# Attention plus MLP on one core: the softmax's running maximum over the first 512 keys, with a check and a second program behind it

## The chip, the core and the metric

The kernel runs on one core of a Trainium2 chip. The metric is device time in microseconds. The core's engines run their own instruction streams and meet through semaphores: TensorE (PE, with its weight loads as PEld), VectorE (DVE), ScalarE (ACT), GpSimd (POOL), and SyncE (SP), whose queue issues all the transfers here.

## The reference

One input `x` of 2048 rows of 448 is normalized row by row, and the normalized rows go through an attention with 16 query heads and a single key and value head of 28 columns, and through an MLP. The output is the sum of `x` and both:

```
xn = layernorm(x)
q = (xn @ wq), 16 heads of 28;  k = xn @ wk;  v = xn @ wv
p = softmax(q k^T * 28**-0.5)            # over 2048 keys
a = (p v, heads joined) @ wo
m = relu(xn @ w1) @ w2                   # 448 -> 1792 -> 448
out = x + a + m
```

The inputs are normal numbers of spread 0.05. A softmax does not change when any one number is taken off a row's scores, as long as the exponentials stay in range. The row's maximum is the usual choice of that number.

## The kernel before, in words

Everything stays in one program without loops at run time. Three stages follow each other.

*Projections.* `x` is normalized and transposed, and q, k and v are computed for four blocks of 512 rows. Each float32 operand is split into a high and a low part, and several matmuls make up for the precision. q, k and v are written to a scratch tensor in DRAM (`qscr`).

*MLP.* The hidden 1792 columns are cut into 7 parts of 256, each over 4 row blocks: 28 tasks (`mlp_up`, `mlp_down`). Max tiles of the attention are mixed into the later tasks, one at each of 12 places of a task (`between`, `one_max`). `LEAD` says how many go here.

*Attention.* The work is cut into 16 units (`NU`): a block of 512 queries by a group of 4 heads. For a unit, a stack `qst` [128, 4, 512] is loaded from `qscr` (`load_stack`: one transfer of zeros and four of q). Its first 112 partitions hold q as high and low parts against the same parts of k in `kst`. Two more partitions hold the negated row maxima as high and low parts against ones in `kst`, so the score matmul itself subtracts the maximum. There are five stack buffers, and unit u + 4 is loaded at the start of unit u, into the buffer that unit u - 1 has given up.

Three kinds of matmul fill TensorE there:

- A **max tile** (`max_tile`, L353): 128 queries by 512 keys of one head into a PSUM bank of the ring `psM` (tile `m`, 4 banks), which VectorE reduces to a row's maximum (L357). Four key blocks, four query blocks and four heads make 64 tiles a unit, 1024 in all. When a unit has all of them, `max_all` and `max_rows` negate, split, transpose and write them into the unit's stack.
- A **score** (`score`, L593): 128 keys by 512 queries of one head into a bank of the ring `psA` (tile `a`, 3 banks), of which ScalarE takes the exponential into a tile `p` (L595). 64 a unit, 1024 in all.
- The products **with v** (`pv`, L477): the four heads of a key block side by side in the array's columns, accumulated over a unit's 16 key blocks in one bank (`psO`). A ones column in `vtile` gives the denominator as row 28 of each head. The trace has two records for each of these 1024 matmuls.

The denominators go by transfer into a tile `d`, are inverted (`recips`), spread and multiplied in (`normalized`), and after each four units the output projection runs (`o_proj`, L530), the last block's in pieces (`o_proj_part`, L546; `finish`).

The order in attention is written by a planner at build time (the loop at the end). It keeps a modelled clock for TensorE (`t`), ScalarE (`act`) and VectorE (`dve`) and the time at which each bank comes free, and it picks next a score, a max tile, a group of v products or an output projection. It paces the max tiles over the scores (`due`, `SLACK`), asks only whether a stack's load has been ordered (`mx_todo[0][0] in qst`), and has no time for transfers. A score takes a bank of `psA`, and one of `psM` only when no max tile is left.

Of the kernel before, what the change touches and what calls it, by code (L numbers as in the profile page):

```python
# [7 lines left out]

F32 = mybir.dt.float32
F32R = mybir.dt.float32r  # L10
AF = mybir.ActivationFunctionType
ALU = mybir.AluOpType
AX = mybir.AxisListType
# [4 lines left out]

@with_exitstack
def attention_plus_mlp(ctx: ExitStack, tc: tile.TileContext, x, wq, wk, wv, wo, w1, w2, out):
    nc = tc.nc
    P = 128
    S, D = x.shape
    DH = wk.shape[1]
# [3 lines left out]
    QB = 512  # L30
    NQB = S // QB
    TPB = QB // P
    HG = 4
# [13 lines left out]
    NU = NQB * NHG  # L47
    NA, NM = 3, 4
    assert DR == 64 and KQ + 2 <= P and HG * 32 == P and NPART * FP == DFF

    ctx.enter_context(tc.manual_schedule())
    cst = ctx.enter_context(tc.tile_pool(name="cst", bufs=1))
    small = ctx.enter_context(tc.tile_pool(name="small", bufs=2))
    dram = ctx.enter_context(tc.tile_pool(name="dram", bufs=1, space=DRAM))
# [12 lines left out]
    vtile = cst.tile([P, NKB, 32], F32, name="vtile")  # L67
# [5 lines left out]
    eps_t = cst.tile([P, 1], F32, name="eps_t")  # L73
    nc.vector.memset(eps_t, EPS)
    warm = cst.tile([P, 1], F32, name="warm")

    pw = psM.tile([P, QB], F32, name="m")
    for _ in range(WARM):
# [243 lines left out]
    def v_rows():  # L322

        pv = psM.tile([P, QB], F32, name="m")
        for kb in range(NKB):
            nc.tensor.transpose(pv[:, kb * 32 : kb * 32 + DH], vT[0][:, kb * P : (kb + 1) * P], ident[0:DH, 0:DH])
        nc.vector.tensor_copy(vtile[:, :, 0:DH], pv.rearrange("p (i d) -> p i d", d=32)[:, :, 0:DH])


    qst, nmx, mx_todo = {}, {}, []  # L330
# [10 lines left out]
            src = qscr[g, r % 2, 0:MQ, b * QB : (b + 1) * QB].rearrange("(j d) q -> d j q", d=DH)  # L341
            nc.sync.dma_start(st.bitcast(F32)[r * DH : (r + 1) * DH], src)

    mx_todo = [(u, j, s, h) for u in range(NU) for j in range(HG) for s in range(TPB) for h in range(4)]

    def max_tile():

        u, j, s, h = mx_todo.pop(0)
        if u not in nmx:
            nmx[u] = small.tile([P, HG * TPB, 4], F32, name="nmx")  # L350
        pm = psM.tile([P, QB], F32, name="m")
        k0 = h * QB
        nc.tensor.matmul(  # L353
            pm, qst[u][0:KQ, j, s * P : (s + 1) * P], kst[0:KQ, k0 : k0 + QB], start=True, stop=True
        )
        n = j * TPB + s
        nc.vector.tensor_reduce(nmx[u][:, n, h : h + 1], pm, axis=AX.X, op=ALU.max)  # L357
        return u if n == HG * TPB - 1 and h == 3 else None

    def max_all(u):  # L360

# [53 lines left out]

    LEAD, PER = 192, 12
    tasks = [(p, b) for p in range(NPART) for b in range(NQB)]
    FIRST = len(tasks) - LEAD // PER  # L420
    pending = []

    def one_max():
        done = max_tile()
        if done is not None:
            pending.append((n + 1, done, max_all(done)))

# [18 lines left out]
        mlp_down(*tasks[-1], i)  # L446
    while pending:
        max_rows(*pending.pop(0)[1:])
    assert len(mx_todo) == NU * HG * TPB * 4 - LEAD
    mlp.close()  # L450


# [51 lines left out]
    def recips(u):  # L504

        r = opool.tile([P, EQ], F32, name="r")
        nc.vector.reciprocal(r, o_r[u])
        nc.sync.dma_start(rscr[u].rearrange("j (g e) -> (j g) e", e=EQ), r)
        rb = opool.tile([P, QB], F32, name="rb")
        for j in range(HG):  # L510
            nc.sync.dma_start(rb[32 * j : 32 * j + 32], rscr[u, j : j + 1].to_broadcast([32, QB]))
        o_r[u] = rb
# [37 lines left out]
    def finish(u):  # L550

        b, g = units[u]
        o = o_acc.pop(u)
        cols = [slice(i * P, (i + 1) * P) for i in range(TPB)]
        oS = opool.tile([P, QB], F32, name="oS")
        on = opool.tile([P, QB], F32, name="on")
        r = opool.tile([P, TPB, HG, 1], F32, name="r")
        rb = opool.tile([P, TPB, HG, 32], F32, name="rb")
        pt = [psA.tile([P, QB], F32, name="a") for _ in cols]
        for i, c in enumerate(cols):  # L560
            nc.scalar.activation(oS[:, c], o[:, c], AF.Copy)
        for i, c in enumerate(cols):
            nc.tensor.transpose(pt[i][:, 0:P], oS[:, c], ident)
            dens = pt[i][:, 0:P].rearrange("p (j c) -> p j c", j=HG)[:, :, DH : DH + 1]
            nc.vector.reciprocal(r[:, i], dens)
            nc.gpsimd.tensor_scalar(rb[:, i], r[:, i].to_broadcast([P, HG, 32]), 1.0, 0.0, op0=ALU.mult, op1=ALU.add)
        for i, c in enumerate(cols):
            pb = psM.tile([P, QB], F32, name="m")
            nc.tensor.transpose(pb[:, 0:P], rb[:, i].rearrange("p j c -> p (j c)"), ident)
            nc.vector.tensor_tensor(on[:, c], pb[:, 0:P], oS[:, c], op=ALU.mult)  # L570
        for i, c in enumerate(cols):
            t = b * TPB + i
            py = psA.tile([P, QB], F32, name="a")
            nc.tensor.matmul(py[:, 0:D], on[:, c], g3[:, g, :], start=True, stop=True)
            nc.vector.tensor_tensor(acc[:, t, :], py[:, 0:D], acc[:, t, :], op=ALU.add)
            nc.sync.dma_start(out[t * P : (t + 1) * P, :], acc[:, t, :])

# [25 lines left out]
    while n_s < n_all or blocks:  # L605
        step = n_s // HG
        room = n_s < n_all and n_open < P_BUFS
        n_max = left - len(mx_todo)
        due = min(left, n_s * left // spread_over)
        wants = mx_todo and n_max < due + SLACK and mx_todo[0][0] in qst  # L610
        rest = rings["M"][0] - t
        pool = "M" if not mx_todo and not fill and rings["M"][0] < rings["A"][0] else "A"
        wait_s = max(0, rings[pool][0] - t) if room and (n_max + SLACK >= due or not wants) else None
        wait_m = max(0, rest) if wants else None
        n_v = ready()
        tail = NKB - blocks[0][1] if blocks else 0
        if n_v < tail <= MIN_V + 1 and room:
            n_v = 0
        least = min((w for w in (wait_s, wait_m) if w is not None), default=None)
        if least == 0:  # L620
            if wait_s == 0 and wait_m == 0:
                what = "S" if act <= dve else "M"
            else:
                what = "S" if wait_s == 0 else "M"
        elif fill and rest <= WAIT and (not mx_todo or what != "F"):
            what = "F"
        elif n_v >= MIN_V or n_v >= 2 and (least is None or least > WAIT) or n_v and (n_s == n_all or not room):
            what = "V"
        elif wait_s is None and wait_m is None:
            if not n_v:  # L630
                t = max(blocks[0][3], t if blocks[0][1] else acc_free)
            what = "V"
            n_v = max(1, ready())
        else:
            what = "S" if wait_m is None or wait_s is not None and wait_s <= wait_m else "M"
        if what == "V" and fill and (len(fill) > 4 * TPB or n_s == n_all and n_v == len(blocks)):
            what = "F"
        if what == "S":
            t = max(t, rings[pool][0])
            assert n_s // (HG * NKB) not in nmx  # L640
            u, kb, p = score(pool)
            n_s += 1
            n_open += 1
            act = max(act + T_EXP, t + TO_ACT)
            rings[pool] = rings[pool][1:] + [act + ACT_OUT]
            t += T_MM
            ps.append(p)
            if len(ps) == HG:
                blocks.append((u, kb, ps, act + ACT_OUT))
                ps = []  # L650
                if kb == 0 and u:
                    load_stack(u + 4)
                for f, a in side.pop(step, ()):
                    f(*a)
        elif what == "M":
            t = max(t, rings["M"][0])
            done = max_tile()
            dve = max(dve + T_MAX, t + TO_DVE)
            rings["M"] = rings["M"][1:] + [dve + DVE_OUT]
            t += T_MM  # L660
            if done is not None:
                dve += T_MAX
                at(step + 1, max_rows, done, max_all(done))
        elif what == "V":
            for u, kb, pp, _ in blocks[:n_v]:
                pv(step, u, kb, pp)
                t += T_PV
                n_open -= HG
                if kb == NKB - 1:
                    act = max(act, t) + T_EXP  # L670
                    acc_free = act + ACT_OUT
            t += T_MODE
            blocks = blocks[n_v:]
        else:
            f, a = fill.pop(0)
            f(*a)
            t = max(t, rings["M"][0]) + 3 * NHG * T_PROJ
            dve = max(dve, t) + T_MAX
            rings["M"] = rings["M"][1:] + [dve + DVE_OUT]
# [26 lines left out]
```

## Time and profile before

| | |
|---|---|
| median of three runs | 1136.87 us (1136.49 to 1138.59) |
| span of the profiled execution, first to last instruction | 1136.1 us |
| first score to last product with v | 389.9 to 1125.5 us |
| TensorE, VectorE, ScalarE busy | 1122.3, 792.7, 589.7 us |
| max tiles on TensorE, reductions on VectorE | 1024, 1024 |
| mean granted clock of TensorE | 0.999 |

The profiled execution is known by its span, 0.8 us under the median; device time is that of the whole execution. Times in the profile count from the span's start. A group's mean is the length of one instruction from its start to its modelled end, and matmuls overlap in the array, so the price of a matmul is read from the distance of the starts.

### The profile page before, as it was taken

To read this page: it belongs to the slowest core of one execution; us is meant where nothing else is said; L and a number is where in the kernel's file an instruction comes from. 1 tells how busy PE (TensorE), PEld (TensorE's weight loads), DVE (VectorE), ACT (ScalarE), POOL (GpSimd) and SP (SyncE) were. 2 spreads that over 40 slices of the span, in tenths; PEclk is the share of its full clock that TensorE was granted. 3 is DMA by queue.
4 is the path that set the end of the run, shared out by engine and by line. 5 is a ranking of instruction groups with operands and counts; after the bars stand their busy time and mean duration, and the time that the engine had idled before them with its cause. 6 is when DMAs were issued, how large, how long until landed. Compare 5 with 4: busy or idle time off the path is not lost.

```text
span 1136.1 us, 15337 instructions
## 1 busy us (share of the span) xinstructions
PE 1122.3 (99%) x5908; PEld 754.4 (66%) x5908; DVE 792.7 (70%) x1385; ACT 589.7 (52%) x1175; POOL 112.7 (10%) x97
## 2 busy tenths in 40 slices
PE   8899999999999999999999999999999999999998
PEld 7688888888888855555556565555665555665553
DVE  6633346888888887788777787777777778767401
ACT  5421111000110277777776676676667767756893
POOL 2204022020200020010110101101010110101110
PEclk9999999999999999999999999999999999999999
DMA  6673810001000102022022110202202020000000
GB/s 217 223 186 68 167 47 1 1 1 36 1 1 1 30 1 48 1 47 39 11 47 49 24 38 18 47 7 50 55 10 52 5 47 9 11 28 9 11 10 33
DMA packets 38478, 47.90 MB, mean 42 GB/s; under 512 B 10294, under 2 KB 25046, under 8 KB 38238
## 3 DMA queue, kind: packets, MB, share of 16 engines
q1 hardware_dynamic: 38406, 46.93, 16.9%
q8 instruction: 46, 0.75, 0.3%
q14 instruction: 26, 0.21, 0.1%
HBM read 32.37 MB, written 12.18 MB: 39 GB/s over the span
## 4 chain that ended last, share of the span: by engine, by line
PE 93%; ACT 3%; DVE 2%; DMA 1%; issue 1%; SPq 0%; DVEq 0%; ACTq 0%
PE m L353 21%; PE a L593 21%; PE o L477 20%; PE a L169 11%; PE a L407 9%; PE o L407 3%; PE m L530 3%; PE a L174 2%; ACT p L595 2%; PE m L593 1%; DMA qscr<-qs 1%; DVE st L182 1%; DMA stg<-in_A_wq 1%; PE m L546 0%; DVE qs L237 0%
## 5 line engine op out<-in xcount | busy, mean ns | idle before, releaser
L357 DVE TENSOR_REDUCE nmx<-m 128x1 f32<-128x512 f32 x1024 | 633.3, 682 | 148.9 <-PE m L353 148.0
L595 ACT ACTIVATE p<-a 128x512 f32<-128x512 f32 x969 | 495.5, 644 | 174.2 <-PE a L593 174.0
L353 PE MATMUL m<-kst,qst 112*128 112x512 f32 x1024 | 407.1, 401 | 0.0
L593 PE MATMUL a<-qst,kst 128*128 128x512 f32 x969 | 388.7, 408 | 0.8 <-ACT p L595 0.5
L593 PEld LDWEIGHTS a<-qst,kst 128*128 128x128 f32 x969 | 183.1, 189 | 117.9 <-issue 55.3
L477 PE MATMUL o<-p,vtile 128*32 128x512 f32 x2048 | 238.6, 596 | 0.0
L353 PEld LDWEIGHTS m<-kst,qst 112*128 112x128 f32 x1024 | 193.8, 189 | 52.2 <-DVE nmx L357 11.4
L394 ACT ACTIVATE hH<-a 128x512 fp32r<-128x512 f32 x56 | 33.5, 598 | 267.4 <-PE a L174 143.0
L477 PEld LDWEIGHTS o<-p,vtile 128*32 128x32 f32 x2048 | 57.6, 109 | 130.6 <-issue 125.1
L169 PE MATMUL a<-xH,w 128*128 128x512 f32 x414 | 112.0, 393 | 3.1 <-ACT xH L225 2.3
L407 PE MATMUL a<-w,hH 128*128 128x448 f32 x336 | 96.0, 367 | 0.0
L169 PEld LDWEIGHTS a<-xH,w 128*128 128x128 f32 x414 | 77.4, 188 | 20.0 <-ACT xH L225 3.1
L395 DVE SCALAR_TENSOR_TENSOR hL<-a,hH 128x512 fp32r<-128x512 f32 x56 | 38.7, 692 | 69.6 <-ACT hH L394 69.6
L516 POOL TENSOR_TENSOR on<-rb,oS 128x512 f32<-128x512 f32 x15 | 19.4, 1292 | 645.7 <-ACT p L595 353.5
L407 PEld LDWEIGHTS a<-w,hH 128*128 128x128 f32 x336 | 63.6, 189 | 8.6
L169 PE MATMUL a<-xL,w 128*128 128x512 f32 x207 | 63.9, 392 | 0.0
L414 DVE TENSOR_TENSOR acc<-a,acc 128x448 f32<-128x448 f32 x84 | 51.8, 618 | 14.8 <-PE a L407 14.8
L407 PE MATMUL a<-w,hL 128*128 128x448 f32 x168 | 61.4, 365 | 0.0
L169 PEld LDWEIGHTS a<-xL,w 128*128 128x128 f32 x207 | 38.9, 188 | 8.8 <-DVE xL L226 0.3
L174 PE MATMUL a<-xR,w 128*128 128x512 f32 x138 | 42.6, 390 | 0.2 <-DVE xR L231 0.2
L595 ACT ACTIVATE p<-m 128x512 f32<-128x512 f32 x55 | 36.2, 741 | 7.0 <-PE m L593 7.0
L407 PEld LDWEIGHTS a<-w,hL 128*128 128x128 f32 x168 | 31.6, 188 | 2.5
(104 smaller groups left out, 539.4 us busy)
## 6 DMA issues: line engine op xcount, KB each, us to landing
qst<-qscr SPq DMA_DIRECT2D x64, 224.0 KB
qscr<-qs SPq DMA_DIRECT2D x16, 512.0 KB
rb<-rscr SPq DMA_DIRECT2D x60, 64.0 KB
acc<-in_A_x SPq DMA_DIRECT2D x16, 224.0 KB
out<-acc SPq DMA_DIRECT2D x16, 224.0 KB
stg<-in_B_w SPq DMA_DIRECT2D x7, 448.0 KB
stg<-in_B_w SPq DMA_DIRECT2D x7, 384.0 KB
qst<-zeros SPq DMA_DIRECT2D x16, 112.0 KB
```

The costliest lines, as they stand in the source:

```text
L169: nc.tensor.matmul(ps, lhs[:, wi, c, cols], xm[:, c, xs], start=n == 0, stop=False)
L174: nc.tensor.matmul(ps, lhs[:, wi, DC, cols], xR[:, xs], start=False, stop=wi == 1)
L353: nc.tensor.matmul(pm, qst[u][0:KQ, j, s * P : (s + 1) * P], kst[0:KQ, k0 : k0 + QB], start=True, stop=True)
L357: nc.vector.tensor_reduce(nmx[u][:, n, h : h + 1], pm, axis=AX.X, op=ALU.max)
L394: nc.scalar.activation(hH[:, f], ph, AF.Relu)
L395: nc.vector.scalar_tensor_tensor(hL[:, f], ph, 0.0, hH[:, f].bitcast(F32), op0=ALU.max, op1=ALU.subtract)
L407: nc.tensor.matmul(py[:, 0:D], hm[:, f, i * P : (i + 1) * P], wd[:, wi, f, :], start=n == 0, stop=n == 3 * FC - 1)
L414: nc.vector.tensor_tensor(acc[:, t, :], py[:, 0:D], acc[:, t, :], op=ALU.add)
L477: nc.tensor.matmul(o_acc[u][32 * j : 32 * j + 32], vtile[:, kb, :], p, start=kb == 0, stop=kb == NKB - 1)
L530: nc.tensor.matmul(py[:, 0:D], om[:, i * P : (i + 1) * P], wm[:, g, :], start=n == 0, stop=n == 3 * NHG - 1)
L593: nc.tensor.matmul(pt, kst[:, kb * P : (kb + 1) * P], qst[u][:, j, :], start=True, stop=True)
L595: nc.scalar.activation(p, pt, AF.Exp, scale=SCALE)
```

## The change

The maximum is taken over the first 512 keys only: `HM` = 1 key block instead of 4, so 16 max tiles a unit and 256 in all. What is subtracted then may be smaller than a row's true maximum. The program sums up what could have gone out of range: all denominators (`dsum`, and `gone` in `finish`), and 1e5 times the largest absolute v. One matmul with a column of ones adds that over the partitions, and a comparison with 1e20 gives an integer `fine`. Every engine reads `fine` into a register. If it is zero, the whole program runs again from the inputs with `HM` = 4, that is, as before. The second program stands behind the first in the code. If `fine` is not zero, every engine branches past it.

Three more things follow from `HM`. `LEAD` falls from 192 to 80 max tiles ahead of attention, which are now five units' tiles instead of three, put into tasks 21 to 27 instead of 12 to 27. A score may take a bank of `psM` at any time (`spare`). And the planner paces 176 max tiles over the scores where it paced 832.

```diff
+def attention_plus_mlp(ctx: ExitStack, tc: tile.TileContext, *io):
...
+    program(tc, 1, fine, *io)
+    flag = nc.values_load(fine, skip_runtime_bounds_check_because="it is only compared with zero")
+    with tc.If(flag == 0):
+        program(tc, 4, None, *io)
...
+            nc.vector.tensor_reduce(
+                gone[:, TPB : TPB + 1], vtile[:, :, 0:DH], axis=AX.XY, op=ALU.max, apply_absolute_value=True
+            )
...
-    mx_todo = [(u, j, s, h) for u in range(NU) for j in range(HG) for s in range(TPB) for h in range(4)]
+    mx_todo = [(u, j, s, h) for u in range(NU) for j in range(HG) for s in range(TPB) for h in range(HM)]
...
-    LEAD, PER = 192, 12
+    LEAD, PER = min(192, 5 * HG * TPB * HM), 12
...
+            nc.vector.tensor_tensor(dsum, dsum, o_r[u], op=ALU.add)
...
+                nc.vector.tensor_reduce(gone[:, i : i + 1], dens, axis=AX.XY, op=ALU.add)
...
+            nc.vector.tensor_reduce(gone[:, TPB + 1 : TPB + 2], dsum, axis=AX.X, op=ALU.add)
+            nc.vector.scalar_tensor_tensor(
+                gone[:, TPB + 1 : TPB + 2], gone[:, TPB : TPB + 1], 1e5, gone[:, TPB + 1 : TPB + 2],
+                op0=ALU.mult, op1=ALU.add,
+            )
+            nc.vector.tensor_reduce(gone[:, TPB : TPB + 1], gone[:, 0:TPB], axis=AX.X, op=ALU.add)
...
+            nc.tensor.matmul(pg[0:1, 0:1], gone[:, TPB : TPB + 1], gone[:, TPB + 2 : TPB + 3], start=True, stop=True)
+            nc.vector.tensor_scalar(fine, pg[0:1, 0:1], 1e20, None, op0=ALU.is_le)
...
-        pool = "M" if not mx_todo and not fill and rings["M"][0] < rings["A"][0] else "A"
+        spare = HM == 1 or not mx_todo and not fill
+        pool = "M" if spare and rings["M"][0] < rings["A"][0] else "A"
```

The change moves instructions. In the order of TensorE after the change (the lines there are 377 for a max tile, 635 for a score, 501 for v, 572 for the last output projection), the place where unit 1 begins: `qst_1279`, `qst_1285` and `qst_3224` are the stacks of units 0, 1 and 5.

```order
L635 MATMUL a_3204<-qst_1279,kst_130 128x512
L635 MATMUL a_3208<-qst_1285,kst_130 128x512
L635 MATMUL a_3212<-qst_1285,kst_130 128x512
L635 MATMUL m_3216<-qst_1285,kst_130 128x512
L635 MATMUL m_3220<-qst_1285,kst_130 128x512
L377 MATMUL m_3231<-kst_130,qst_3224 128x512
L377 MATMUL m_3234<-kst_130,qst_3224 128x512
L377 MATMUL m_3237<-kst_130,qst_3224 128x512
L501 MATMUL o_2963<-p_3130,vtile_88 32x512
```

The first max tile of unit 5 stands four scores behind the last score of unit 0, whose buffer unit 5 takes over. The same place on SP's queue, after the change:

```order
L404 DMA qst_1303<-rows_2879 1x16x128 x2
L487 DMA wo_2893<-in_A_wo 28x4x448 x4
L363 DMA qst_3224<-zeros_90 14x16x128
L366 DMA qst_3224<-qscr_131 28x4x512 x4
L525 DMA d_3258<-oS_3256 32x1x16 x4
```

Unit 5's stack is loaded ahead of unit 0's denominators (`d`). Before the change the first max tile of unit 5 (its stack is `qst_3737`) stood in the middle of unit 2 (`qst_1282`), on TensorE:

```order
L353 MATMUL m_4319<-kst_122,qst_1294 128x512
L593 MATMUL a_4322<-qst_1282,kst_122 128x512
L353 MATMUL m_4326<-kst_122,qst_1294 128x512
L593 MATMUL a_4334<-qst_1282,kst_122 128x512
L353 MATMUL m_4339<-kst_122,qst_3737 128x512
L593 MATMUL a_4342<-qst_1282,kst_122 128x512
L477 MATMUL o_4346<-p_4229,vtile_84 32x512
```

There it was the 140th score's neighbour, 76 scores behind the last of unit 0. Scores and max tiles stood in turn there, and after the change up to nine scores stand together, in banks `a` and `m`.

The end of attention on TensorE, before:

```order
L546 MATMUL m<-woH,oL 128x448
L477 MATMUL o<-p,vtile 32x512 x24
L593 MATMUL m<-qst,kst 128x512 x2
L593 MATMUL a<-qst,kst 128x512 x3
L593 MATMUL m<-qst,kst 128x512 x4
L593 MATMUL a<-qst,kst 128x512 x3
L593 MATMUL m<-qst,kst 128x512 x4
L477 MATMUL o<-p,vtile 32x512 x16
L563 MATMUL a<-ident,oS 128x128 x4
```

and after:

```order
L635 MATMUL m<-qst,kst 128x512 x2
L635 MATMUL a<-qst,kst 128x512 x2
L572 MATMUL m<-woH,oH 128x448
L572 MATMUL m<-woL,oH 128x448
...
L501 MATMUL o<-p,vtile 32x512 x20
L589 MATMUL a<-ident,oS 128x128 x4
L597 MATMUL m<-ident,rb 128x128 x4
L612 MATMUL a<-wo,on 128x448 x4
L617 MATMUL m<-gone 1x1
```

The last 16 scores stood behind the pieces of the output projection and a long v group. Now the last scores stand ahead of 27 matmuls of that projection, and one small matmul for the flag follows the program's last. Over the whole order, v products come in 95 groups instead of 89, and in 289 of the 1024 scores no max tile stands between their v group and the one before it.

More of the change, by code (lines that the diff above doesn't have):

```diff
@@ L10 @@
 F32R = mybir.dt.float32r
+I32 = mybir.dt.int32
 AF = mybir.ActivationFunctionType
@@ L21, in attention_plus_mlp, with program @@
 @with_exitstack
-def attention_plus_mlp(ctx: ExitStack, tc: tile.TileContext, x, wq, wk, wv, wo, w1, w2, out):
+def attention_plus_mlp(ctx: ExitStack, tc: tile.TileContext, *io):
+    nc = tc.nc
+    ctx.enter_context(tc.manual_schedule())
+    keep = ctx.enter_context(tc.tile_pool(name="keep", bufs=1))
+    fine = keep.tile([1, 1], I32, name="fine")
+    program(tc, 1, fine, *io)
+    flag = nc.values_load(fine, skip_runtime_bounds_check_because="it is only compared with zero")
+    with tc.If(flag == 0):
+        program(tc, 4, None, *io)
+@with_exitstack
+def program(ctx: ExitStack, tc: tile.TileContext, HM, fine, x, wq, wk, wv, wo, w1, w2, out):
     nc = tc.nc
@@ L49, in attention_plus_mlp @@
     assert DR == 64 and KQ + 2 <= P and HG * 32 == P and NPART * FP == DFF
-    ctx.enter_context(tc.manual_schedule())
     cst = ctx.enter_context(tc.tile_pool(name="cst", bufs=1))
@@ L75, in attention_plus_mlp @@
     warm = cst.tile([P, 1], F32, name="warm")
+    dsum = cst.tile([P, QB * HG // P], F32, name="dsum")
+    nc.vector.memset(dsum, 0.0)
+    gone = cst.tile([P, TPB + 3], F32, name="gone")
+    nc.vector.memset(gone, 1.0)
     pw = psM.tile([P, QB], F32, name="m")
@@ L327, in v_rows @@
         nc.vector.tensor_copy(vtile[:, :, 0:DH], pv.rearrange("p (i d) -> p i d", d=32)[:, :, 0:DH])
+        if fine is not None:
+            nc.vector.tensor_reduce(
+                gone[:, TPB : TPB + 1], vtile[:, :, 0:DH], axis=AX.XY, op=ALU.max, apply_absolute_value=True
+            )
     qst, nmx, mx_todo = {}, {}, []
@@ L349, in max_tile @@
         if u not in nmx:
-            nmx[u] = small.tile([P, HG * TPB, 4], F32, name="nmx")
+            nmx[u] = small.tile([P, HG * TPB, HM], F32, name="nmx")
         pm = psM.tile([P, QB], F32, name="m")
@@ L357, in max_tile @@
         nc.vector.tensor_reduce(nmx[u][:, n, h : h + 1], pm, axis=AX.X, op=ALU.max)
-        return u if n == HG * TPB - 1 and h == 3 else None
+        return u if n == HG * TPB - 1 and h == HM - 1 else None
     def max_all(u):
@@ L414, in mlp_down @@
         nc.vector.tensor_tensor(acc[:, t, :], py[:, 0:D], acc[:, t, :], op=ALU.add)
-    LEAD, PER = 192, 12
+    LEAD, PER = min(192, 5 * HG * TPB * HM), 12
     tasks = [(p, b) for p in range(NPART) for b in range(NQB)]
-    FIRST = len(tasks) - LEAD // PER
+    FIRST = len(tasks) - -(-LEAD // PER)
     pending = []
     def one_max():
-        done = max_tile()
+        done = max_tile() if len(mx_todo) > NU * HG * TPB * HM - LEAD else None
         if done is not None:
@@ L448, in attention_plus_mlp @@
         max_rows(*pending.pop(0)[1:])
-    assert len(mx_todo) == NU * HG * TPB * 4 - LEAD
+    assert len(mx_todo) == NU * HG * TPB * HM - LEAD
     mlp.close()
@@ L507, in recips @@
         nc.vector.reciprocal(r, o_r[u])
+        if fine is not None:
+            nc.vector.tensor_tensor(dsum, dsum, o_r[u], op=ALU.add)
         nc.sync.dma_start(rscr[u].rearrange("j (g e) -> (j g) e", e=EQ), r)
@@ L565, in finish @@
             nc.vector.reciprocal(r[:, i], dens)
+            if fine is not None:
+                nc.vector.tensor_reduce(gone[:, i : i + 1], dens, axis=AX.XY, op=ALU.add)
             nc.gpsimd.tensor_scalar(rb[:, i], r[:, i].to_broadcast([P, HG, 32]), 1.0, 0.0, op0=ALU.mult, op1=ALU.add)
@@ L570, in finish @@
             nc.vector.tensor_tensor(on[:, c], pb[:, 0:P], oS[:, c], op=ALU.mult)
+        if fine is not None:
+            nc.vector.tensor_reduce(gone[:, TPB + 1 : TPB + 2], dsum, axis=AX.X, op=ALU.add)
[4 more added lines that the diff above has]
+            nc.vector.tensor_reduce(gone[:, TPB : TPB + 1], gone[:, 0:TPB], axis=AX.X, op=ALU.add)
+            nc.vector.tensor_tensor(
+                gone[:, TPB : TPB + 1], gone[:, TPB : TPB + 1], gone[:, TPB + 1 : TPB + 2], op=ALU.add
+            )
         for i, c in enumerate(cols):
@@ L576, in finish @@
             nc.sync.dma_start(out[t * P : (t + 1) * P, :], acc[:, t, :])
+        if fine is not None:
+            pg = psM.tile([P, QB], F32, name="m")
+            nc.tensor.matmul(pg[0:1, 0:1], gone[:, TPB : TPB + 1], gone[:, TPB + 2 : TPB + 3], start=True, stop=True)
+            nc.vector.tensor_scalar(fine, pg[0:1, 0:1], 1e20, None, op0=ALU.is_le)
     T_MM, T_PV, T_MODE, T_EXP, T_MAX, T_PROJ = 235, 860, 370, 478, 598, 203
```

## The prediction

> **What bounds the kernel now.** I read the page's busy times and its chain of waits first:
>
> ```profile
> PE 1122.3 (99%) x5908; PEld 754.4 (66%) x5908; DVE 792.7 (70%) x1385; ACT 589.7 (52%) x1175; POOL 112.7 (10%) x97
> ...
> PE 93%; ACT 3%; DVE 2%; DMA 1%; issue 1%; SPq 0%; DVEq 0%; ACTq 0%
> PE m L353 21%; PE a L593 21%; PE o L477 20%; PE a L169 11%; PE a L407 9%; PE o L407 3%; PE m L530 3%; PE a L174 2%; ACT p L595 2%; PE m L593 1%; DMA qscr<-qs 1%; DVE st L182 1%; DMA stg<-in_A_wq 1%; PE m L546 0%; DVE qs L237 0%
> ```
>
> TensorE carries 93% of the chain, and the max tiles (L353) are 21% of it by themselves. VectorE is 70% busy, but it ends only 2% of the waits: its reductions of those tiles run beside TensorE. The attention stage alone, from the first score to the last product with v, in the view of busy time by stretch (us; busy PE, PEld, DVE, ACT, POOL with counts; clock; DMA):
>
> ```profile
> 389.90:1125.50 735.60, 733.76 (x4098) 424.58 (x4097) 526.79 (x903) 523.25 (x1053) 55.37 (x48) 1.00 0.12 27
> ```
>
> So TensorE is the bound in the 735.6 us of attention, and ScalarE, with 523 us, is next if TensorE loses enough. The groups by line give what is to be removed:
>
> ```profile
> L357 DVE TENSOR_REDUCE nmx<-m 128x1 f32<-128x512 f32 x1024 | 633.3, 682 | 148.9 <-PE m L353 148.0
> ...
> L353 PE MATMUL m<-kst,qst 112*128 112x512 f32 x1024 | 407.1, 401 | 0.0
> ```
>
> The 401 ns is a matmul's length in the pipe, not its price. The price is the distance from start to start. The timeline of TensorE (start, length):
>
> ```profile
> 501.01 0.39 PE L593 MATMUL a<-qst,kst 128*128 128x512 f32 x1
> 501.33 2.78 PE L477 MATMUL o<-p,vtile 128*32 128x512 f32 x24
> 504.05 0.50 PE L593 MATMUL a<-qst,kst 128*128 128x512 f32 x1
> 504.38 0.40 PE L353 MATMUL m<-kst,qst 112*128 112x512 f32 x1
> 504.62 0.40 PE L593 MATMUL a<-qst,kst 128*128 128x512 f32 x1
> ...
> 508.57 0.49 PE L353 MATMUL m<-kst,qst 112*128 112x512 f32 x1
> ```
>
> From 504.62 to 508.57 stand 17 steps, scores and max tiles in turn: 3.95 / 17 = 0.232 us for either.
>
> **Part 1: 768 of 1024 max tiles go.** Of the 832 in attention 176 stay, so 656 go, each at 0.232 us of the bounding engine: **-152.5 us**. The other 112 go from the MLP (192 to 80). There the price is the period of one MLP task without and with its 12 tiles, from the chain in order of time:
>
> ```profile
> 74.44 1.21 PE a L407 x6
> ...
> 84.32 1.21 PE a L407 x6
> ...
> 192.26 0.93 PE a L169 x4
> ...
> 205.02 0.93 PE a L169 x4
> ```
>
> 84.32 - 74.44 = 9.88 us, 205.02 - 192.26 = 12.76 us, so 2.88 / 12 = 0.24 us a tile: **-26.9 us**. The reductions that go with them were under TensorE's cover and bring nothing more.
>
> **Part 2: the order that follows.** The products with v come in groups, and each group costs a change of the array's shape. In the chain:
>
> ```profile
> 395.27 1.85 PE o L477 x16
> ...
> 711.91 3.57 PE o L477 x32
> ```
>
> 16 records (two key blocks) take 1.85 us and 32 take 3.57, so a block is 0.86 us. In the timeline, a score at 501.01 and a group of three blocks take until 504.05, 3.04 us: less 0.23 for the score and 2.58 for the blocks leaves 0.23, and the first score after it takes 0.33 instead of 0.23: 0.33 us a group. The order has 95 groups where it had 89: **+2.0 us**.
>
> **Part 3: a wait that was not there.** Units 5 to 9 now ask for their maxima right behind the order to load their stack (the order shown with the change). A max tile reads the stack, so TensorE, which issues in order, stands until the load lands; behind it on TensorE stand a group of v products and the next scores, and ScalarE, behind those, empties the seven banks and stands too. How long a load takes shows in SP's queue (start, issue time) and the DMA share of the microseconds behind it (eighth and ninth figure: DMA share, GB/s):
>
> ```profile
> 439.53 0.90 SPq L339 DMA_DIRECT2D qst<-zeros  x1
> 440.47 2.27 SPq L342 DMA_DIRECT2D qst<-qscr  x4
> ...
> 484.57 0.90 SPq L339 DMA_DIRECT2D qst<-zeros  x1
> ```
>
> ```profile
> 446.00:447.00 1.00, 1.00 (x6) 0.69 (x4) 1.00 (x2) 1.00 (x4) 0.00 (x0) 1.00 0.94 165
> 447.00:448.00 1.00, 1.00 (x8) 0.41 (x10) 1.00 (x3) 1.00 (x4) 0.00 (x0) 1.00 0.46 64
> ...
> 492.00:493.00 1.00, 1.00 (x6) 0.83 (x5) 1.00 (x3) 1.00 (x3) 0.00 (x0) 1.00 0.53 83
> ```
>
> Issue begins at 439.53 and 484.57, traffic ends near 447.5 and 492.5: 8.0 us, and I allow 0.4 for the signal, 8.4 us. The load may start when the last score of the unit five back has run. By the order, TensorE's own work between that score and the tile is 4 scores (1 us) for units 5 and 6; 7 scores and 4 blocks (5.1 us) for 7 and 8; 8.5 us for 9; 12 scores and 3 blocks and some (5.8 us) for 10; from unit 11 on over 14 us. The waits are 7.4 + 7.4 + 3.3 + 3.3 + 0 + 2.6 = **+24 us**. In these stretches TensorE has no slack (part 4), so all of it lengthens the span. Ends: 0 if the load lands before the tile, and 6 x 8.4 = 50 if none of that work covers it; I take the count, since it follows from the order and two loads that agree. On SP the load now stands ahead of the copies of the denominators instead of behind them, so nothing delays it there. Before, unit 5's tiles came 76 scores behind the earliest start of its load.
>
> After long idling the clock drops. In the stretch at the end where TensorE does nothing:
>
> ```profile
> 1132.00:1136.00 4.00, 0.00 (x0) 0.00 (x0) 0.56 (x1) 0.00 (x0) 0.00 (x0) 0.82 0.47 171
> ```
>
> The clock is 0.82 over 4 us, 0.72 us of full speed lost. I charge each of the two long waits that: **+1.4 us** (from 0, if it comes back at once, to 8, if four waits each bring 4 us at half speed). [...]
>
> **Part 4: TensorE and ScalarE tie where no tiles stand.** 289 of the 1024 scores now stand in groups without a max tile. The end of the old kernel has such a stretch, with scores in both rings of banks:
>
> ```profile
> 1069.54 0.50 PE L593 MATMUL a<-qst,kst 128*128 128x512 f32 x1
> ...
> 1087.88 16.67 ACT p L595 x34
> ...
> 1099.52 0.51 PE L593 MATMUL a<-qst,kst 128*128 128x512 f32 x1
> ```
>
> 34 exponentials in 16.67 us are 0.490 each. TensorE's price for a score there is 0.232 + 0.86 / 4 + 0.33 / 8 = 0.489: a tie. From 1069.54 to 1099.52, 61 scores, 15 blocks and 7 groups take 29.98 us against 14.2 + 12.9 + 2.3 = 29.4 by price: 0.6 us lost on 61, 0.0097 a score. Times 289: **+2.8 us**. The lower end is 0, the upper one stands in part 5. Elsewhere the tiles and the output projection keep TensorE ahead: 523 us of ScalarE in some 612.
>
> **Part 5: both ends of the last unit.** At the end of the old order 16 scores waited for ScalarE's banks behind a long v group:
>
> ```profile
> 1116.73 0.73 PE L593 MATMUL m<-qst,kst 128*128 128x512 f32 x2
> ...
> 1122.32 4.05 PE L477 MATMUL o<-p,vtile 128*32 128x512 f32 x32
> ```
>
> 5.59 us for 16 scores, 1.9 more than their price, or 0.117 each (as much for each of the 289 scores of part 4 would be 34 us, the upper end there). In the new order the output projection (27 matmuls in a row) stands behind the last scores and covers their exponentials: **-1.9 us** (0 to -4).
>
> The check adds, on VectorE's tail, four reductions between the reciprocals and four small operations behind them; the nearest rows:
>
> ```profile
> 1127.15 0.85 DVE L565 RECIPROCAL r<-a 128x4 f32<-128x4 f32 x4 [14.98 <-PE a L563]
> ...
> 1129.68 2.88 DVE L575 TENSOR_TENSOR acc<-a,acc 128x448 f32<-128x448 f32 x4 [0.39 <-PE a L574]
> 1130.34 2.59 SPq L576 DMA_DIRECT2D out<-acc  x4
> ```
>
> A small operation is 0.85 / 4 = 0.21 us. Three reductions stand ahead of the last reciprocal and four operations ahead of the additions, of which 0.4 was idle anyway: 1.0 us. Then the flag: a matmul, a comparison, a read into every engine's register and a jump over the second program. The output needs 1136.1 - 1132.9 = 3.2 us from its last issue to the end, which covers as much; bounds from there: 0, and two more such trips to memory, 6.4 us, for register and code. I take 2, since most lies under the output's landing: **+3.0 us** in all. [...] The accumulation of the sums (15 additions) and the maximum of v, 0.2 to 0.7 us each, lie on VectorE, which loses 768 reductions of 0.62 us.
>
> **Sum.** Against the profiled span: 1136.1 - 152.5 - 26.9 + 2.0 + 24 + 1.4 + 2.8 - 1.9 + 3.0 = 988.0 us. The median 1136.87 is 0.8 above that span, so **989 us**, 13% less.
>
> **The rivals.**
> *The loads are in time* (TensorE gets there later than its bare work says, or a tile waits for less). For it: scores that wait for ScalarE's banks delay the first tile. Against it: 1 us against 8.4. Then 24 and 1.4 go: 963 us.
> *Max tiles queue behind exponentials.* Scores may now take the banks of the tiles' ring, so a tile's bank may be waiting for ScalarE. If half of the 176 tiles wait one exponential beyond their price (0.49 - 0.23 = 0.26 us), that is +23: 1012 us. For it: ScalarE with 523 us in 612 often has a full queue. Against it: the order is made with both rings' due times.
> *The flag is zero.* Then the second program runs whole, and no part of it overlaps with the first: 989 + 1136 = 2125 us, slower than before. It decides as soon as one denominator's sum passes 1e20 or is no number. The inputs speak against it: normalized rows and weights of spread 0.05 make scores of spread near 1, so a maximum over 512 keys misses the full one by a few units, and e to a few units is far from 1e20. The profile of before cannot show it.
>
> **How the numbers follow.** Forecast 67%, loads in time 15%, tiles behind exponentials 15%, flag zero 3%. The forecast alone spans 974 to 1004: half the loads' wait either way, and 3 us for the small ends. The range takes in both neighbours, 960 to 1016. Faster by over 0.2% (what a measurement here tells from no change) 97%, within it 0%, slower 3%.
>
> **What would show it.** Max tiles number 256, and MLP tasks without tiles last until the 21st. The first score starts near 363 us. Around the first scores of units 1 and 2 TensorE idles some 7 us in front of a max tile, released by the stack's load, around 3 and 4 about 3 us; later units show none. The clock dips there alone. Busy ScalarE stays under 90% of attention. After the last output no more than some 4 us pass. The prediction is wrong if TensorE idles by over 20 us elsewhere, or if its idle time in front of max tiles is released by exponentials.

## The result

The changed kernel takes 1036.32 us (1035.49 to 1037.53) where the kernel before takes 1137.04: a ratio of 0.911 (0.910 to 0.913). The forecast was 989 us in a range of 960 to 1016. So the sign was right and 47 us of the expected 148 did not come. The profiled execution took 1036.39 us, with a span of 1034.6.

The page of the changed kernel, busy times and the chain that ended last:

```profile
PE 972.1 (94%) x5142; PEld 621.4 (60%) x5142; DVE 338.9 (33%) x644; ACT 586.7 (57%) x1175; POOL 112.5 (11%) x97
...
PE 83%; DMA 6%; ACT 5%; issue 2%; SPq 2%; DVE 2%; ACTq 0%; DVEq 0%
```

TensorE's share of the chain fell from 93% to 83%. Transfers, SP's queue and ScalarE came in. TensorE now idles 62 us where it idled 14. Attention, from the first score to the last product with v, in the view by stretch:

```profile
364.33:1021.00 656.67, 608.53 (x3441) 311.57 (x3439) 136.82 (x256) 519.50 (x1051) 55.14 (x48) 0.97 0.14 30
```

It starts at 364.3 (forecast near 363) and takes 657 us, where the terms of the prediction add up to 611. So nearly all that is missing is here. The groups of max tiles and their reductions:

```profile
L381 DVE TENSOR_REDUCE nmx<-m 128x1 f32<-128x512 f32 x256 | 170.2, 686 | 419.1 <-PE m L377 418.8
...
L377 PE MATMUL m<-kst,qst 112*128 112x512 f32 x256 | 107.8, 427 | 40.0 <-DMA qst<-qscr 36.5
```

The 256 tiles are there, and TensorE stood 36.5 us in front of them for the stack's load. Two of these places, in the timelines of TensorE and of SP's queue (start, length, and in brackets the idle time before and what ended it):

```profile
394.64 0.99 PE L635 MATMUL m<-qst,kst 128*128 128x512 f32 x2
403.89 1.62 PE L377 MATMUL m<-kst,qst 112*128 112x512 f32 x3 [8.26 <-DMA qst<-qscr]
405.44 4.72 PE L501 MATMUL o<-p,vtile 128*32 128x512 f32 x32
...
580.51 2.44 SPq L525 DMA_DIRECT2D d<-oS  x4
583.05 0.90 SPq L363 DMA_DIRECT2D qst<-zeros  x1
583.99 2.32 SPq L366 DMA_DIRECT2D qst<-qscr  x4
592.51 1.19 PE L377 MATMUL m<-kst,qst 112*128 112x512 f32 x2 [11.70 <-DMA qst<-qscr]
```

The first is unit 5, as forecast, 8.26 us against 7.4. The last line is unit 9, for which the prediction had no wait: there the load stood behind the four copies of the denominators on SP, which had to wait for ScalarE's copy of the accumulator (0.60 us, from 579.89). The six waits are 8.3, 7.7, 2.6, 3.6, 11.7 and 2.7 us, for units 5 to 10. Behind 8.26 us of standing, 32 records with v take 4.72 us. They take 3.57 in the kernel before, at a clock of 1.00 (at 711.91). The clock of these stretches (seventh figure of a row):

```profile
400.00:450.00 50.00, 38.42 (x210) 18.36 (x210) 10.54 (x21) 32.45 (x66) 3.20 (x3) 0.88 0.18 36
...
550.00:600.00 50.00, 37.80 (x210) 21.18 (x208) 8.59 (x17) 29.20 (x60) 3.19 (x3) 0.86 0.16 37
...
592.50:602.00 9.50, 9.48 (x36) 5.95 (x37) 3.45 (x7) 5.39 (x11) 0.00 (x0) 0.67 0.01 2
```

In the 9.5 us after unit 9's wait, with TensorE busy throughout, the mean clock is 0.67. It is 0.50 from 592.51 to 598.80 and 1.00 from there to 602.00, so 6.3 of the 9.5 us were slow. Behind unit 5's wait, from 403.89 to 407.70, the mean clock is 0.50 as well.

### The profile page after: what moved, and what is told of

Same layout as the page of the kernel before. It is cut to its first block, busy times and chain, and to the rows that moved or that the text cites. A ratio compares the mean times of both kernels' runs of the same rounds, so it can differ in the third digit from the quotient of the medians.

```text
span 1034.6 us, 13287 instructions
## 1 busy us (share of the span) xinstructions
PE 972.1 (94%) x5142; PEld 621.4 (60%) x5142; DVE 338.9 (33%) x644; ACT 586.7 (57%) x1175; POOL 112.5 (11%) x97
## 4 chain that ended last, share of the span: by engine, by line
PE 83%; DMA 6%; ACT 5%; issue 2%; SPq 2%; DVE 2%; ACTq 0%; DVEq 0%
PE o L501 20%; PE a L189 12%; PE a L635 12%; PE m L635 12%; PE a L431 10%; PE m L377 6%; ACT p L637 4%; DMA qst<-qscr 4%; PE o L431 3%; PE m L556 3%; PE a L194 3%; SPq L366 1%; DMA qscr<-qs 1%; DVE st L202 1%; DMA stg<-in_A_wq 1%
## 5 line engine op out<-in xcount | busy, mean ns | idle before, releaser
L637 ACT ACTIVATE p<-a 128x512 f32<-128x512 f32 x504 | 303.2, 692 | 61.8 <-PE a L635 61.5
L637 ACT ACTIVATE p<-m 128x512 f32<-128x512 f32 x520 | 311.8, 711 | 36.8 <-PE m L635 36.5
L381 DVE TENSOR_REDUCE nmx<-m 128x1 f32<-128x512 f32 x256 | 170.2, 686 | 419.1 <-PE m L377 418.8
L501 PE MATMUL o<-p,vtile 128*32 128x512 f32 x2048 | 242.4, 603 | 0.0
L635 PE MATMUL a<-qst,kst 128*128 128x512 f32 x504 | 186.6, 421 | 3.1 <-ACT rows L400 2.7
L635 PE MATMUL m<-qst,kst 128*128 128x512 f32 x520 | 187.4, 417 | 1.9 <-ACT rows L400 0.9
L377 PE MATMUL m<-kst,qst 112*128 112x512 f32 x256 | 107.8, 427 | 40.0 <-DMA qst<-qscr 36.5
L635 PEld LDWEIGHTS a<-qst,kst 128*128 128x128 f32 x504 | 95.3, 192 | 71.9 <-ACT p L637 42.9
L635 PEld LDWEIGHTS m<-qst,kst 128*128 128x128 f32 x520 | 97.2, 190 | 67.9 <-ACT p L637 33.0
L377 PEld LDWEIGHTS m<-kst,qst 112*128 112x128 f32 x256 | 49.9, 197 | 70.0 <-issue 47.8
```

What stands on the lines that cost most here:

```text
L377: nc.tensor.matmul(pm, qst[u][0:KQ, j, s * P : (s + 1) * P], kst[0:KQ, k0 : k0 + QB], start=True, stop=True)
L501: nc.tensor.matmul(o_acc[u][32 * j : 32 * j + 32], vtile[:, kb, :], p, start=kb == 0, stop=kb == NKB - 1)
L635: nc.tensor.matmul(pt, kst[:, kb * P : (kb + 1) * P], qst[u][:, j, :], start=True, stop=True)
L637: nc.scalar.activation(p, pt, AF.Exp, scale=SCALE)
```

## The experiments

Part of the question can be read from the traces without a run. By the prediction's prices (0.232 us a score or tile, 0.86 a block, 0.33 a group) and two more from the traces (0.20 a projection matmul, from start to start, and 0.3 for a unit's transpose) TensorE's work in attention is 721 us before and 570 after. It took 736.9 and 657.5. So 16 us were not in the prices before, and 87 are not now. The question is what the other 71 are: loads, the clock, ScalarE, or the order. The two runs on the check and the flag, and the one that fills the waits, change the changed kernel itself. All the others are built on the kernel of the first experiment, which holds the tiles back, and their differences are counted from it unless said otherwise.

### Max tiles asked for later

```diff
+        wants = wants and n_s >= asked.get(mx_todo[0][0], -99) + HOLD
...
                     load_stack(u + 4)
+                    asked[u + 4] = n_s
```

`HOLD` is 32, and `asked` holds the score at which a stack's load was ordered. The order that follows has 100 groups of v products instead of 95.

> The planner asks for a unit's max tiles only from 32 scores after it has ordered the unit's stack, some 16 us, so that no tile meets an unfinished load; the work is otherwise the same. Theory (waits for loads, and the slow clock after them): the 36 us of idle TensorE in front of max tiles and the slow stretches behind them go, about 36 + 13 us, to about 987 us, and no granted clock under 1.00 is left in attention. Rival (ScalarE ties with TensorE, and only the place of the waiting changes): ScalarE's bound shows instead and at most 20 us come back, 1015 us or more.

Measured: 996.55 us (996.29 to 997.50), ratio 0.876 (0.875 to 0.878), 39.8 us less than the changed kernel. Attention:

```profile
364.10:982.10 618.00, 603.23 (x3441) 305.38 (x3439) 136.02 (x256) 518.74 (x1053) 55.24 (x48) 1.00 0.14 32
```

The clock is 1.00, and no wait for a load is left. So loads and clock cost 39.8 us, where the theory said 49. 46 us over the prices (572) remain, 30 more than before the change. In that remainder the views of waits of this kernel, and of the kernel before (waiter, releaser, total us, times, longest):

```profile
PEld m L636 <- ACT p L638: 50.3, 102, 1.8
PEld a L636 <- ACT p L638: 45.9, 93, 1.3
...
PEld m L377 <- ACT p L638: 16.7, 28, 1.3
```

```profile
PEld a L593 <- ACT p L595: 29.8, 114, 0.8
...
PEld m L593 <- ACT p L595: 4.8, 11, 0.8
```

The weight loads, which run ahead of the matmuls (by 0.23 us in the changed kernel where one starts at 433.96 and its matmul at 434.19), wait 113 us for exponentials, where they waited 35. Mostly it is scores that wait for a bank, not tiles. One such stretch on TensorE, 16 scores in a row between two groups of v products:

```profile
430.98 0.50 PE L636 MATMUL a<-qst,kst 128*128 128x512 f32 x1
...
433.15 0.98 PE L636 MATMUL a<-qst,kst 128*128 128x512 f32 x2
434.12 1.49 PE L636 MATMUL m<-qst,kst 128*128 128x512 f32 x3
...
436.50 3.64 PE L501 MATMUL o<-p,vtile 128*32 128x512 f32 x32
```

The first ones go at their price. From 433.15 on they start 0.49 us apart, which is what one exponential takes. The 16 take 5.52 us, and their price is 3.7.

### Work in place of the wait

```diff
+        if HM == 1 and j == 0 and s == 0:
+            for _ in range({5: 31, 6: 29, 8: 11, 9: 46}.get(u, 0)):
+                nc.tensor.matmul(pm, kst[:, 0:P], kst[:, 0:QB], start=True, stop=True)
```

> Ahead of the first max tile of units 5, 6, 8 and 9, 31, 29, 11 and 46 matmuls that nobody reads go into the tile's own bank (0.232 us each, a little under the wait they stand in). The waits for the loads stay as long; TensorE is not idle in them. Theory (the clock falls behind a long idle stretch and costs time of its own): the granted clock stays 1.00 in attention and 10 to 15 us come back, about 1024 us. Rival (the slow stretches cost nothing beyond the waits, since ScalarE is behind then anyway): the clock stays up and the time stays within 3 us of 1036.

Measured: 1029.07 us (1028.50 to 1029.76), ratio 0.905 (0.904 to 0.906): 7.2 us less. The same stretches as above:

```profile
400.00:450.00 50.00, 47.58 (x256) 26.23 (x255) 10.70 (x22) 32.45 (x66) 3.19 (x3) 1.00 0.19 36
...
550.00:600.00 50.00, 48.30 (x276) 29.11 (x265) 9.38 (x18) 30.37 (x63) 3.96 (x4) 1.00 0.16 37
```

The clock stays up, and the time falls. The waits are no shorter: the fillers and the idle time left in front of the tiles add up to 36.8 us, where the waits were 36.5. So the slow clock has a price of its own, between what the two theories said (10 to 15 us, and under 3). It is at least the 7.2 us seen, since unit 10's wait, 3.3 us here, brought a dip that the changed kernel does not have there (from 600 to 650 the clock is 0.97 here and 1.00 there). It is at most the full speed lost in the rows behind the four waits of the changed kernel, about 10.7 us (1.9, 2.7, 3.0 and 3.1). Of the 39.8 us, then, some 7 are the clock and 33 the waits themselves.

### Without the check and the second program

```diff
-    program(tc, 1, fine, *io)
-    flag = nc.values_load(fine, ...)
-    with tc.If(flag == 0):
-        program(tc, 4, None, *io)
+    program(tc, 1, None, *io)
```

> The first program alone: no sums, no flag, no register read, no second program behind it. Theory (the check costs what the end of the span shows, 13.6 us after the last product with v against 10.1): 3 to 5 us less, 1032 us. Rival (a branch past a whole program costs a fetch that the span does not show): 8 us less or more, under 1029 us. If the check were all under the output's landing, 1036 us.

Measured: 1033.14 us (1030.24 to 1035.37), ratio 0.908 (0.907 to 0.910): 3.2 us less, as the theory had it, with executions that spread more than the others'. Of the profiled execution 1.7 us lie outside the span, where the changed kernel has 1.8. This leaves no room for a large cost that the span does not show.

### The flag at zero

```diff
-            nc.vector.tensor_scalar(fine, pg[0:1, 0:1], 1e20, None, op0=ALU.is_le)
+            nc.vector.tensor_scalar(fine, pg[0:1, 0:1], -1.0, None, op0=ALU.is_le)
```

> The comparison is with -1 instead of 1e20, so the flag is zero and the second program, with the maximum over all keys, runs behind the first. Theory (nothing overlaps, as the prediction has it): 1036 + 1136 = 2172 us, within 10. Rival (the second program's first loads and weights start while the first one's output lands, or its clock is warm): 2160 us or less.

Measured: 2165.39 us, one execution, within the 10 us that the theory gave. The second program begins behind the flag in the timeline:

```profile
1027.68 0.13 DVE L618 TENSOR_SCALAR fine<-m 1x1 int32<-1x1 f32 x1
1030.17 0.82 SPq L79 DMA_DIRECT2D acc<-in_A_x  x2
```

It takes 2163.6 - 1030.2 = 1133.4 us, so the two programs follow each other. Compared with it, the jump can be read. Here, where the branch is not taken, the next program's first transfer is issued 2.5 us after the flag. The profile puts the start of the other engines there (GpSimd at 1030.19) down to the first program's output transfers, so reading the flag takes 2.5 us at most. In the changed kernel, where the branch is taken, the flag and the end of the output's issue stand here:

```profile
1025.54 2.42 SPq L614 DMA_DIRECT2D out<-acc  x4
...
1027.52 0.13 DVE L618 TENSOR_SCALAR fine<-m 1x1 int32<-1x1 f32 x1
```

The span ends at 1034.6, 7.0 us after the flag and 6.6 us after the last issue of the output. The kernel before ended 3.2 us after its own, and the run without the check 2.8. So the flag and the taken jump together cost 3.4 us that the output does not cover, counted against the kernel before (3.8 against the run without the check). How much is the jump and how much the read of the flag, no run here separates.

### Half of every exponential

```diff
-        nc.scalar.activation(p, pt, AF.Exp, scale=SCALE)
+        nc.scalar.activation(p[:, 0:256], pt[:, 0:256], AF.Exp, scale=SCALE)
...
-                o_acc[u][32 * j : 32 * j + 32], vtile[:, kb, :], p, ...
+                o_acc[u][32 * j : 32 * j + 32], vtile[:, kb, :], p[:, None, 0:256].to_broadcast([P, 2, 256]), ...
```

> As the kernel that holds the tiles back 32 scores (996.6 us), but ScalarE takes the exponential of 256 of a score's 512 columns, and the products with v read those 256 twice; half of the softmax is left out, TensorE's instructions keep their number, order and size. What is left of attention over TensorE's own prices there is 46 us, where the kernel before had 16. Theory A (TensorE waits for ScalarE, which nearly ties with it): those 30 us go, about 967 us. Theory B (the excess is in the order, the shared banks of tiles and scores or TensorE's own switching): under 8 us go, 988 us or more.

Measured: 963.49 us (962.58 to 963.52), 33.1 less. ScalarE's pieces and what is left of the weight loads' waits for them:

```profile
L638 ACT ACTIVATE p<-m 128x256 f32<-128x256 f32 x521 | 183.9, 406 | 89.7 <-PE m L636 85.3 <-PE a L636 2.6
```

```profile
PEld m L636 <- ACT p L638: 12.7, 22, 0.9
...
PEld m L377 <- ACT p L638: 5.2, 11, 0.8
...
PEld a L636 <- ACT p L638: 2.8, 4, 0.8
```

This kernel leaves out the exponentials of half the queries, so its output is not the softmax. 113 us of waits became 21, with TensorE's instructions unchanged. Attention takes 584.9 us against 571.9 by prices, 13 over, which is what the kernel before had. Theory A holds: the 33 us were TensorE waiting for ScalarE. Theory B falls.

### The small copies on VectorE

```diff
-            nc.scalar.activation(oS, o_acc.pop(u), AF.Copy)
+            nc.vector.tensor_copy(oS, o_acc.pop(u)) if HM == 1 else nc.scalar.activation(oS, o_acc.pop(u), AF.Copy)
...
-        nc.scalar.activation(rows, pn[0 : 2 * n, 0:P], AF.Copy)
+        nc.vector.tensor_copy(rows, pn[0 : 2 * n, 0:P]) if HM == 1 else nc.scalar.activation(rows, pn[0 : 2 * n, 0:P], AF.Copy)
```

(In the first program only. The planner counts the copy of the accumulator on VectorE.)

> As the kernel that holds the tiles back (996.6 us), with the copies of the v accumulator (15, 0.6 us each) and of the maxima's rows (16, 0.26 us) on VectorE instead of ScalarE, some 12 us less for ScalarE in attention. Theory A (ScalarE ties): 6 to 12 us less, about 987 us. Theory B: within 3 us of 996.6.

Measured: 989.95 us (989.13 to 991.11), ratio 0.870 (0.869 to 0.872): 6.6 less than the kernel that holds the tiles back, and the fastest of the versions that leave nothing out, 46 us under the change. It is at the low end of theory A and outside B.

### Five banks for scores alone

```diff
-    NA, NM = 3, 4
+    NA, NM = (5, 2) if HM == 1 else (3, 4)
...
-        spare = HM == 1 or not mx_todo and not fill
+        spare = not mx_todo and not fill
```

> As the kernel that holds the tiles back (996.6 us), with five banks for the scores alone and two for tiles and output projections, none shared while tiles are left. Theory A (ScalarE ties; seven banks against five matter little): 996 to 1003 us. Theory C (tiles queue behind exponentials in the shared ring): 10 us less or more, under 987 us.

Measured: 1016.73 us (1016.24 to 1017.11), ratio 0.894 (0.892 to 0.895): 20.2 slower. About 5.7 of it lies ahead of attention (the first stages use the rings too, and the first score starts at 369.8 instead of 364.1), and 14.5 in attention. The weight loads of scores now wait this long for exponentials:

```profile
PEld a L636 <- ACT p L638: 142.8, 364, 0.8
```

So parting tiles and scores costs more than it saves, theory C falls, and theory A was wrong on the size. In the shared rings tiles do queue behind exponentials, but with 16.7 of the 113 us they are the smaller part. That it is the scores' five banks against seven is argued: this run also left two banks to tiles and output projections, and the tiles' weight loads wait 13.5 us for reductions where they waited 5.2.

### No v group over three blocks

```diff
+        n_v = min(n_v, 3) if HM == 1 else n_v
         if what == "V" and fill and ...
```

> As the kernel that holds the tiles back (996.6 us), with no group of v products over three key blocks (2.9 us of TensorE; seven full banks are 3.4 us of work for ScalarE): groups of 4 to 6 blocks are cut, and the number of groups goes from 100 to 105 (5 x 0.33 us). Theory D (ScalarE runs dry behind long groups, and that time does not come back): 5 to 10 us less, about 989 us. Theory A without D: 997 to 999 us.

Measured: 1001.88 us (999.86 to 1002.33), ratio 0.880 (0.879 to 0.882): 5.3 slower. Theory D falls, and the 997 to 999 us of A without D were missed too. Five groups more account for 1.7 us of it; the rest is unexplained.

### The old rule for banks

```diff
-        spare = HM == 1 or not mx_todo and not fill
+        spare = not mx_todo and not fill
```

> As the kernel that holds the tiles back (996.6 us), with the bank rule of before: scores take the three banks of their own ring while max tiles are left, and four banks stay with the tiles and projections. Theory A (ScalarE ties, and what it has in full banks while TensorE makes v products decides): three full banks are 1.4 us of work against 2 to 3 us of a v group, so it is clearly slower, 25 to 50 us, 1020 to 1045 us. If tiles that queue behind exponentials cost more than the banks bring, it is faster than 996.

Measured: 1103.22 us (1102.61 to 1104.12), ratio 0.970 (0.969 to 0.972): 106.7 slower than with shared banks, more than twice what was expected. The waits of the weight loads for exponentials, those of ScalarE for scores, and one round of TensorE's timeline:

```profile
PEld a L636 <- ACT p L638: 251.3, 623, 0.8
...
ACT p L638 <- PE a L636: 155.8, 99, 5.3
```

```profile
423.89 1.92 PE L501 MATMUL o<-p,vtile 128*32 128x512 f32 x16
425.74 0.96 PE L636 MATMUL a<-qst,kst 128*128 128x512 f32 x3
426.93 2.46 PE L636 MATMUL a<-qst,kst 128*128 128x512 f32 x5 [0.22 <-ACT p L638]
429.32 1.92 PE L501 MATMUL o<-p,vtile 128*32 128x512 f32 x16
```

Three scores go at full pace into the three banks, and the next five take 2.46 us, 0.49 each, ScalarE's pace. Then ScalarE, with at most three full banks, runs dry during the v group. It waits 155.8 us for scores over the whole kernel, where it waits 84 with shared banks. A round of eight scores takes 429.32 - 423.89 = 5.43 us, where its price is 8 x 0.232 + 2 x 0.86 + 0.33 = 3.91. So one line of the change, the shared banks, carries most of the gain: without it, fewer max tiles bring 3%, even with no wait for loads. The bank rule is that of before here, and attention is some 148 us over its prices, where the kernel before had 16.

### Longer v groups

```diff
-    left, SLACK, MIN_V, WAIT = len(mx_todo), 6, 3, 50
+    left, SLACK, MIN_V, WAIT = len(mx_todo), 6, 4 if HM == 1 else 3, 50
```

(On top of the copies on VectorE.)

> As the kernel with the copies on VectorE (989.95 us), with v products asked for in groups of four key blocks instead of three where the order allows it: 95 groups instead of 97, 20 of four blocks instead of 13. Theory A (TensorE and ScalarE tie; longer groups let ScalarE run dry, fewer save 0.33 us each): within 4 us of 990, slower if the dry stretches win. If group changes were the cost, faster by the 0.7 us of two groups.

Measured: 995.86 us (995.39 to 996.43), ratio 0.876 (0.874 to 0.877): 5.9 slower than the copies alone. That is outside the 4 us of the expectation, on the side of the dry stretches. Shorter groups (the run with the cap) and longer ones both cost 5 to 6 us against the planner's order. Whether three is the best setting, two neighbours do not show.

## Why the prediction was wrong

By its own steps:

- **Part 1 held in its price.** The MLP's gain came but for 1.3 us: attention starts 25.6 us earlier, where the term was 26.9. The first 50 us had a clock of 0.97 in this execution, where the kernel before had 1.00; the attention of the kernel that holds the tiles back starts at 364.1, 0.2 us earlier. How much of the 1.3 us is the clock was not shown. That 656 tiles at 0.232 us left the attention is shown by the two sums of prices, 721 and 570, and by the run with half exponentials, in which attention follows the prices as closely as before.
- **Part 2 held**: 95 groups.
- **Part 3 had the mechanism right and its size too low.** TensorE stood 36.5 us, of which the runs show 33 in the time, where the term was 24, and the clock cost 7 where its term was 1.4. The first miss is unit 9: it was given no wait, because of 8.5 us of work on TensorE ahead of its tile, and stood 11.7 us. The other five waits were within 1 us of their terms, though a load took longer than the 8.4 us charged: 9.4 to 9.9 us from the first issue to the tile. Of the 8.4, the 0.4 for the signal stood on no row. The sentence that "the load now stands ahead of the copies of the denominators" was read from unit 5 and does not hold for unit 9, where the order had it the other way round. On the clock, the price was taken from a stretch in which TensorE did nothing, and charged for two waits alone. Four waits had a slow stretch behind them, the shortest of them a wait of 3.6 us (a clock of 0.50 for 5.9 us behind it). 7.2 us over four waits is 1.8 each, where the price was 0.7. That mean hides the single waits: the row behind unit 9's lost 3.1 us.
- **Part 4 failed, and it is the largest miss.** It charged 2.8 us for the tie of TensorE and ScalarE (where no tiles stand, both need about 0.49 us a score), 289 scores at what a calm stretch of 61 had lost, and said that elsewhere "the tiles and the output projection keep TensorE ahead". Taking ScalarE's work down by nearly half brings 33 us. The excess is spread over all units, with tiles or without: mostly 2 to 4 us a unit over the prices in the kernel that holds the tiles back, where the kernel before had 0.5 to 1.4 in all units but the last. ScalarE's 519 busy microseconds in 618 are no slack that can be had at any moment. It stops while TensorE works off v products and projections (in the changed kernel 1.80 us up to 648.35, behind a v group of 3.64 us, and 1.49 us up to 642.03, behind projections), and TensorE fills seven banks and then goes at 0.49 us a score. Before, a max tile stood between most neighbouring scores (808 of 1023 pairs, against 167 after) and spaced them at 0.465 us, close to ScalarE's own pace. The change took away this spacing, which the prediction did not see as a part of what it removed. That ScalarE costs the 33 us is shown; that the lost spacing is why it costs more than before is argued from the order and from the run with the old bank rule, and no run put other work in the tiles' place. The prediction's own upper end for this term was 34 us, but its range did not take that in, and that it comes near the 33 is in part luck: it was meant for the 289 scores without tiles alone.
- **Part 5 held in its sum**: 3.2 us where 3.0 were charged, but by luck: the reductions cost nothing (the last unit takes 6.1 us from its transposes to the last output issue in both kernels), and flag and jump all of it. That the flag's price is bounded by trips to memory was the author's estimate, and no run shows it. Of the -1.9 us for the last scores, 1.3 came: the last unit is 2.3 us over its prices, where it was 3.6.
- **The rivals.** "Max tiles queue behind exponentials" was nearest in time with 1012 us, but the waits are mostly those of scores, and separate banks are slower. "The loads are in time" described a kernel that the run holding the tiles back built, and the tie took 33 us of it.
- **Its signs of being wrong did not show**, though it was wrong. TensorE idled 11.6 us in attention apart from the loads, under the 20 that were named, and its idle time in front of tiles was ended by loads. What it lost to ScalarE does not show as idle time: the kernel that holds the tiles back has TensorE busy in 603 of 618 us, though its work comes to 572 by the prices. The loss shows in the waits of the weight loads and in the distance of the scores' starts.

The prediction without its loads, clock and tie is 961 us, and the kernel with half exponentials and no waits for loads measured 963.5. From there the runs give 33.1 (ScalarE), 32.6 (loads) and 7.2 (clock) up to the changed kernel; these are differences of runs, so that they close is no evidence by itself. Against the terms, ScalarE was 30 us short, the loads 9, the clock 6, and the rest 3: the 47 us. Why groups of v products of other lengths cost 5 to 6 us each way is open.

## What to carry to other kernels

When work is taken off the bounding engine, add up what the next engine needs and then ask whether the removed work spaced the two: with 519 of 618 us busy, ScalarE cost 33 us, and with three banks between the engines instead of seven the kernel took 107 more. TensorE's busy share, 603 of 618 us, did not show this loss; its time against the sum of its prices, 572 us, did. When a planner moves a consumer closer to the order of a transfer, count the distance to the landing for each place in the order, with what stands ahead on the transfer's queue, because a rule read at one place did not hold at the fifth. Idle stretches of TensorE cost more than their length here, 7 us on top of 33, with the clock at 0.50 behind the four of 3.6 to 11.7 us.

## What was not expected of the hardware

The slow clock outlasted the waits, by different times: 3.8 us of work at a mean clock of 0.50 behind the wait of 8.3 us, and 6.3 us at 0.50 behind the wait of 11.7 us. The waits of 2.6 and 2.7 us in the same execution left the clock at 1.00. And the flag with a taken branch over a whole program cost about 3.4 us that the output did not cover, where the same flag with the branch not taken let the next program's first transfer out after 2.5 us.
